# Attention scores made one tile further ahead, normalisations at the head of a step, halves of unit 0 at its end

## The chip, the cores and the metric

One core of one Trainium2 chip runs the whole program; inputs and outputs lie in device memory. The metric is the device time of one execution in microseconds (us), the median of several runs. Engines, in the names of the profile: PE multiplies matrices, DVE (VectorE) and ACT (ScalarE) work elementwise and can reach PSUM, POOL (GpSimd) works elementwise in SBUF only, SP issues the DMAs. Each takes its instructions in the order in which the program lists them, and semaphores hold an instruction until what it needs is there.

## The reference

```
k_sum = max over 32 keys;  v_sum = mean over 32 values          (24 blocks)
scores_l = q k^T / 8 where |i-j| < 16, else -1e9
scores_s = q k_sum^T / 8 + log 32
a = softmax(concat(scores_l, scores_s));  x = a @ concat(v, v_sum)
x = MoE(x)   8 experts, relu MLP 512-1024-512, gates by 8 Sinkhorn rounds
y = (P(h)/Q(h)) @ w_out,  h = x @ w_in                          1536 tokens
```

Batch 2, 8 heads, 768 positions, head size 64, all float32.

## The kernel before, in words

The first 105 us or so are the attention, run as a software pipeline over 24 tiles of 64 queries (a tile has all 8 heads). The loop at line 866 has steps `s` = 0 to 26. A tile `t` goes through these helpers:

- `scores(t)` (L605): 16 small PE products into the PSUM tile `sc` (one buffer), then four DVE reductions that add the mask and keep each row's minimum (L631). It reads the keys of slot `t` in `kw` and four tiles' queries in `qs`, of which there are two buffers.
- `exps(t)` (L637): four ACT exponentials with row sums.
- `norm(t)` (L645): DVE adds 1e-9 (L651), takes the reciprocal (L652), multiplies (L653). The two small results lie in a spare corner of the newest `xo` PSUM tile up to tile 16, and in the SBUF tile `sm` from tile 17.
- `trans(t)` (L655): four PE transposes, one ACT copy to `aT` (pool `att`, two buffers).
- `av(t)` (L669): 16 PE products into `xo` (one PSUM buffer; tiles 1 and 3 use another pool), then ACT writes `xh` (L687) and DVE `xl` (L688). Then `load_vx` asks SP for the values of tile t+3.

Step `s` of the loop issues scores of tile s, av of tile s-3, trans of tile s-2, norm of tile s-1, exps of tile s. Then follows a list of jobs due at that step (`todo`): transposes and copies of later queries and keys (`prep_q` at steps 6, 10, 14, 18; `prep_k` at 7, 8, 9), keys' block maxima on DVE (`block_keys`, L480, steps 8 to 10), copies of them by POOL into the slots of tiles 12 to 15 (`blocks_to`, step 10), weight splitting on ACT and POOL (`split_w2`, steps 8 and 9), and block means of v. From step 7 on, each step also gets one or two "halves" (`mains`, `share`): six PE products each of the first MoE unit on tokens that are already through; two halves of one step stand apart in steps 7 to 11 (one after `av`, one at the end). The ACT and DVE work of a finished pair waits in `posts` and is issued by `flush` after the next `av`. In steps 3 to 5 `spin(3)` issues three dummy PE products whose result nobody reads.

After the loop come the remaining products of the MoE and the last layer, in an order fixed by the program. The block from L866 to L901 is the one that the change rewrites:

```
if s<NQ: scores(s)          # L869
av(s-AV); load_vx; flush()  # L885
trans(s-AV+1); norm(s-1)    # L891, L895
exps(s); todo; main         # L897
```

Of the kernel before, what the change touches and what calls it, by code (L numbers as in the profile page):

```python
# [22 lines left out]
def kernel(  # L23
# [14 lines left out]
    nc = tc.nc  # L38
    B, H, S, D = q.shape
    NT, DM = out.shape  # L40
    NE, _, FE = w1.shape
# [12 lines left out]
    QT = 64  # L54
    NQ = NT // QT
    QB = S // QT
    BLK, WIN = 32, 16
    NB = S // BLK
    WK = QT + 2 * WIN
    SO = 96  # L60
    CO = SO + NB
    NP = H // 2
    LT = 2 * P
    NL = S // LT
# [301 lines left out]
    with ExitStack() as actx:  # L366
# [4 lines left out]
        NS = 16  # L371
        kw = a1.tile([P, NS, NP, CO], F32, name="kw")
        vx = [a1.tile([CO, DM], F32, name=f"vx{i}") for i in range(3)]
        qs = [a1.tile([P, NP, LT], F32, name=f"qs{i}") for i in range(2)]
        wavg = a1.tile([P, 2 * NB], F32, name="wavg")
# [3 lines left out]
        nat = {}  # L379
        kT = {}  # L380
        ks = {}
        vs = {}
        qT = {}
        st = {}
        vps = {}
# [144 lines left out]
        def prep_q(b, i):  # L530
            new_q(b, i)
            for par in range(2):
                place(qT[b, i], par, transpose8("q", b, i, par), qscale, (b, i) == (0, 2))

        def spin(n):

            ps = psm.tile([P, 512], F32, tag="mm", name=f"spin_{len(spins)}")
            spins.append(n)
            for i in range(n):
                nc.tensor.matmul(ps[:, 0:P], lhsT=ident, rhs=ident, start=True, stop=True)  # L540
# [6 lines left out]
            nc.gpsimd.tensor_add(s, t[:, :, 0, :], t[:, :, 1, :])  # L547
            nat["vsum", b, i] = s

        def prep_v(b, *parts):  # L550
            if parts[0] == 0:
                vps[b] = psm.tile([P, DM], F32, tag="mm", name=f"vps_{b}")
            ps = vps[b]
            nb = LT // BLK
            for i in parts:
                o = (NB - nb) - nb * i
                if i == NL - 1:
                    t = nat.pop(("v", b, i))
                    rs_ = [t[:, :, y, :] for y in range(2)]
                else:  # L560
                    rs_ = [nat.pop(("vsum", b, i))]
                for n, r in enumerate(rs_):
                    nc.tensor.matmul(
                        ps[SO:SO + NB, :].rearrange("p (h d) -> p h d", h=H), lhsT=wavg[:, o:o + NB], rhs=r,
                        start=(i == 0), stop=n == 1, tile_position=(0, SO),
                    )
            if parts[-1] == NL - 1:
                nc.vector.tensor_copy(vx[0][SO:SO + NB, :], ps[SO:SO + NB, :])
                vs[b] = vx[0]

        def means_split(i):
            x = nat.pop(("vsum", 1, i)).rearrange("p h d -> p (h d)")
# [23 lines left out]
        def load_vx(t):  # L596
            b, r = divmod(t, QB)
            lo, hi = r * QT - WIN, r * QT + QT + WIN
            c0, c1 = max(lo, 0), min(hi, S)
            nc.sync.dma_start(  # L600
                vx[t % 3][c0 - lo:c1 - lo, :].rearrange("p (h d) -> p h d", h=H),
                v[b, :, c0:c1, :].rearrange("h p d -> p h d"),
            )

        def scores(t):  # L605
            b, r = divmod(t, QB)
            qt = qT[b, r // TPL]
            if t == 1:
                ps = [psa.tile([P, NP, P], F32, tag="tr", name=f"sc_{t}_{x}", bufs=2) for x in range(2)]
            else:  # L610
                ps = psa.tile([P, 2, NP, P], F32, tag="sc", name=f"sc_{t}")
                ps = [ps[:, x] for x in range(2)]
            w = kw[:, slot(t)]
            i = 0 if r == 0 else (2 if r == QB - 1 else 1)
            m = masks[i]
            o = r % TPL * QT
            for p in range(NP):
                x = p % 2
                p = x * (NP // 2) + p // 2
                for j in range(2):  # L620
                    h = slice(j * D, (j + 1) * D)
                    y = (j ^ x) * D
                    nc.tensor.matmul(
                        ps[x][y:y + D, p % (NP // 2), 0:CO], lhsT=qt[h, p, o:o + QT], rhs=w[h, p, :],
                        start=True, stop=True, tile_position=(j * D, y),
                    )
            a = apool.tile([P, NP, CO], F32, tag="a", name=f"a_{t}", bufs=3)
            sm = apool.tile([P, 4, NP], F32, tag="sm", name=f"sm_{t}", bufs=3)
            for p in range(NP):
                p = p % 2 * (NP // 2) + p // 2  # L630
                nc.vector.tensor_tensor_reduce(  # L631
                    out=a[:, p, :], in0=ps[p // (NP // 2)][:, p % (NP // 2), 0:CO], in1=m[:, 0, :],
                    scale=-1.0, scalar=3.0e38, op0=ALU.add, op1=ALU.min, accum_out=sm[:, 0, p:p + 1],
                )
            st[t] = (a, sm, a)

        def exps(t):  # L637
            a, sm, x = st[t]
            for p in range(NP):
                p = p % 2 * (NP // 2) + p // 2  # L640
                nc.scalar.activation(
                    a[:, p, :], x[:, p, :], AF.Exp, scale=-1.0, bias=sm[:, 0, p:p + 1], accum_out=sm[:, 1, p:p + 1]
                )

        def norm(t):  # L645
            a, sm, _ = st[t]
            e, r = sm[:, 2, :], sm[:, 3, :]
            if t < NS + 1:
                o = st["xo"]
                e, r = o[:, 0, QT:QT + NP], o[:, 1, QT:QT + NP]  # L650
            nc.vector.tensor_scalar_add(e, sm[:, 1, :], 1e-9)  # L651
            nc.vector.reciprocal(r, e)  # L652
            nc.vector.tensor_mul(a, a, r.unsqueeze(2).to_broadcast([P, NP, CO]))  # L653

        def trans(t):  # L655
            a = st.pop(t)[0]
            ps = psa.tile([P, NP * P], F32, tag="tr", name=f"at_{t}", bufs=2)
            for p in range(NP):
                nc.tensor.transpose(ps[0:CO, p * P:(p + 1) * P], a[:, p, :], ident)
            aT = apool.tile([CO, NP * P], F32, tag="aT", name=f"aT_{t}")  # L660
            nc.scalar.copy(aT, ps[0:CO, :])
            st[t, "aT"] = aT
# [6 lines left out]
        def av(t):  # L669
            aT = st.pop((t, "aT"))  # L670
            if t < 4 and t % 2:
                ps = psm.tile([P, NP * P], F32, tag="mm", name=f"xo_{t}").rearrange("p (c n) -> p c n", c=NP)
            else:
                ps = psa.tile([P, NP, P], F32, tag="xo", name=f"xo_{t}")
            for p in range(NP):
                for j in range(2):
                    y = p * P + (j ^ (p >= NP // 2)) * QT
                    nc.tensor.matmul(  # L678
                        ps[j * D:(j + 1) * D, p, 0:QT],
                        lhsT=vx[t % 3][:, (2 * p + j) * D:(2 * p + j + 1) * D],  # L680
                        rhs=aT[:, y:y + QT],
                        start=True, stop=True,
                    )
            st["xo"] = ps
            o = t * QT
            dh, dl = xh[:, :, o:o + QT], xl[:, :, o:o + QT]
            nc.scalar.copy(dh, ps[:, :, 0:QT])  # L687
            nc.vector.tensor_sub(dl, ps[:, :, 0:QT], dh.bitcast(F32))  # L688
# [158 lines left out]
        AV = 3  # L847
        mains = []
# [7 lines left out]
                    mains.append((ready, 0, f, NCH, h))  # L856
        share = dict(zip(range(7, 26), (2, 2, 2, 2, 2, 2, 2, 2, 2, 2, 1, 1, 2, 2, 2, 1, 1, 2, 2)))

        def main(s, end):
            n = share.get(s, 0)  # L860
            apart = n == 2 and s < QB
            for _ in range((1 if apart else n) if end else int(apart)):
                assert mains[0][0] <= s
                mains.pop(0)[2]()

        for s in range(NQ + AV):  # L866
            if s == 2:
                norm(0)
            if s < NQ:  # L869
                scores(s)  # L870
            if s == 2:
                prep_v(0, 0)
                prep_v(0, 1)
                norm(1)
                exps(2)
                trans(0)
                by_token_half(0)
                by_token_half(1)
            if s == AV:
                trans(1)  # L880
                exps(3)
                norm(2)
                prep_v(0, 2)
                prep_q(0, 1)
            if s >= AV:  # L885
                av(s - AV)
                if s - AV + 3 < NQ:
                    load_vx(s - AV + 3)
                flush()
            main(s, False)  # L890
            if AV < s < NQ + AV - 1:  # L891
                trans(s - AV + 1)
            if 2 < s < 6:
                spin(3)
            if AV < s <= NQ:  # L895
                norm(s - 1)
            if s < NQ and s not in (2, AV):  # L897
                exps(s)
            for f in todo.pop(s, []):
                f()  # L900
            main(s, True)  # L901
        assert not todo
        flush()
        assert not mains[0][4]
# [88 lines left out]
    for src, dst in ((w_in, f_in), (w_out, f_out)):  # L993
        rows, cols = dst[0].shape[0] // P, dst[0].shape[1]
        flat, o = rows * cols, 0
        while o < flat:
            e = min(o + CW, flat)
# [461 lines left out]
```

## Time and profile before

| | us |
|---|---|
| median of 3 runs (1351.87 to 1351.96) | 1351.94 |
| the profiled execution | 1352.21 |
| its span, first to last instruction | 1350.5 |

| engine | busy us | share |
|---|---|---|
| PE | 1342.1 | 99% |
| DVE | 1052.9 | 78% |
| POOL | 804.3 | 60% |
| ACT | 510.9 | 38% |

The times of the rows further down are microseconds from the start of the span. In a row of the timeline stand start, busy time, engine, line, operation, output and inputs, and how many instructions were merged; in brackets how long the engine was idle before and what ended that. The end of a PE product is modelled, so neighbouring PE rows overlap: what PE gives to a group is read from one start to the next.

### The profile page before, as it was taken

The numbers are of one execution on the slowest core, as the hardware profiler recorded it, in microseconds if no ns is written. First come the engines' busy times: TensorE is split into PE (matmuls) and PEld (weight loads), VectorE is DVE, ScalarE is ACT, GpSimd is POOL, SyncE is SP. The second block draws the span as 40 slices with busy tenths as digits, with TensorE's granted clock in tenths as the row PEclk, the third lists the DMA queues.
The fourth block names the chain that finished last, engine by engine and source line by source line (L and its number), as shares of the span: only waits on it lengthen the run. The fifth ranks groups of instructions, "written<-read, shape, count | busy, mean of one in ns | idle before, by whom it ended". The sixth has DMA issues, their size and how long they took to land.

```text
span 1350.5 us, 20263 instructions
## 1 busy us (share of the span) xinstructions
PE 1342.1 (99%) x7343; PEld 1186.0 (88%) x7343; DVE 1052.9 (78%) x1956; ACT 510.9 (38%) x1136; POOL 804.3 (60%) x983
## 2 busy tenths in 40 slices
PE   8999999999999999999999999999999999999999
PEld 6888898999999999999999999999999888888887
DVE  7775588777777777777787777777777689988885
ACT  6874313222222222222222222222222379866662
POOL 7625747777776777776777767777777012222221
PEclk9999999999999999999999999999999999999999
DMA  9730112222222222222222222222222411312102
GB/s 262 169 85 1 51 46 63 89 70 79 67 73 68 67 77 67 83 66 87 69 77 72 67 74 68 76 69 77 75 80 62 146 57 47 94 33 94 32 16 78
DMA packets 122004, 102.40 MB, mean 76 GB/s; under 512 B 36272, under 2 KB 102960, under 8 KB 121904
## 3 DMA queue, kind: packets, MB, share of 16 engines
q1 hardware_dynamic: 121904, 101.10, 25.7%
q8 instruction: 58, 0.95, 0.3%
q14 instruction: 42, 0.34, 0.1%
HBM read 81.15 MB, written 19.92 MB: 75 GB/s over the span
## 4 chain that ended last, share of the span: by engine, by line
PE 97%; DVE 1%; DMA 1%; ACT 0%; SPq 0%; issue 0%; POOL 0%; DVEq 0%; ACTq 0%
PE p_v L185 12%; PE p_v L184 12%; PE p_v L186 12%; PE p L184 8%; PE p L186 8%; PE p L185 8%; PE X L1234 6%; PE X L1232 6%; PE X L1233 6%; PE Z L1233 3%; PE Z L1234 3%; PE Z L1232 3%; PE Y L1234 2%; PE Y L1233 2%; PE Y L1232 2%; PE xo L678 1%
## 5 line engine op out<-in xcount | busy, mean ns | idle before, releaser
L1347 DVE SCALAR_TENSOR_TENSOR accs<-p_v,Pt,accs 128x512 f32<-128x512 f32 x336 | 244.4, 746 | 85.9 <-PE p_v L186 85.2
L184 PE MATMUL p_v<-w2h_v,hh_v 128*128 128x512 f32 x720 | 282.2, 392 | 0.1
L186 PE MATMUL p_v<-w2h_v,hl_v 128*128 128x512 f32 x720 | 281.9, 392 | 0.0
L185 PE MATMUL p_v<-w2l_v,hh_v 128*128 128x512 f32 x720 | 281.7, 391 | 0.0
L1241 DVE SCALAR_TENSOR_TENSOR hl_v<-s,hh_v 128x384 fp32r<-128x384 f32 x180 | 137.4, 763 | 76.0 <-ACT hh_v L1240 74.6
L234 POOL TENSOR_TENSOR hl<-ta,hh 128x512 fp32r<-128x512 f32 x48 | 62.5, 1302 | 204.4 <-ACT hh L233 150.0
L1252 ACT COPY s<-X 128x384 f32<-128x384 f32 x56 | 27.0, 482 | 406.6 <-PE X L1234 406.6
L1041 POOL TENSOR_SCALAR ce<-ce 128x296 uint32<-128x296 uint32 (+1 forms) x56 | 67.1, 1199 | 176.7 <-DVE ce L1032 176.7
L186 PEld LDWEIGHTS p_v<-w2h_v,hl_v 128*128 128x128 f32 x720 | 135.2, 188 | 28.3
L184 PEld LDWEIGHTS p_v<-w2h_v,hh_v 128*128 128x128 f32 x720 | 135.4, 188 | 26.3 <-DVE accs L1342 0.5
L185 PEld LDWEIGHTS p_v<-w2l_v,hh_v 128*128 128x128 f32 x720 | 135.3, 188 | 25.9
L1240 ACT ACTIVATE hh_v<-s 128x384 fp32r<-128x384 f32 x180 | 94.9, 527 | 126.8 <-DVE s L1275 68.6
L110 POOL TENSOR_TENSOR wS<-S,wS 128x256 fp32r<-128x256 f32 x120 | 100.2, 835 | 14.4 <-ACT wS L107 4.7
L184 PE MATMUL p<-xh,w1h 128*128 128x512 f32 (+2 forms) x272 | 100.8, 371 | 0.0
L186 PE MATMUL p<-xh,w1l 128*128 128x512 f32 (+2 forms) x272 | 99.1, 364 | 0.0
L185 PE MATMUL p<-xl,w1h 128*128 128x512 f32 (+2 forms) x272 | 99.1, 364 | 0.0
L184 PE MATMUL p<-w2h,hh 128*128 128x512 f32 (+1 forms) x240 | 94.0, 392 | 0.0
L186 PE MATMUL p<-w2h,hl 128*128 128x512 f32 (+1 forms) x240 | 93.3, 389 | 0.0
L185 PE MATMUL p<-w2l,hh 128*128 128x512 f32 (+1 forms) x240 | 93.2, 388 | 0.0
L110 POOL TENSOR_TENSOR w2l_v<-sb,w2h_v 128x512 fp32r<-128x512 f32 x60 | 82.9, 1382 | 5.0
L1234 PE MATMUL X<-th,wS 128*128 128x384 f32 x240 | 80.3, 335 | 0.0
L1232 PE MATMUL X<-th,wS 128*128 128x384 f32 x240 | 80.3, 335 | 0.0
(249 smaller groups left out, 3309.1 us busy)
## 6 DMA issues: line engine op xcount, KB each, us to landing
sa<-in_moe_w_dram SPq DMA_DIRECT2D x30, 512.0 KB, 3.4
sb<-in_moe_w_dram SPq DMA_DIRECT2D x30, 512.0 KB, 4.3
cv<-in_moe_w_in_dram SPq DMA_DIRECT2D x24, 296.0 KB, 2.9
w1h<-f_in SPq DMA_DIRECT2D x16, 256.0 KB, 2.8
w1l<-f_in SPq DMA_DIRECT2D x16, 256.0 KB, 3.2
w2h<-f_out SPq DMA_DIRECT2D x16, 256.0 KB, 4.9
w2l<-f_out SPq DMA_DIRECT2D x16, 256.0 KB, 5.1
vx<-in_v_dram SPq DMA_DIRECT2D x20, 192.0 KB, 4.2
```

Of the source, the lines that this page charges most:

```text
L110: nc.gpsimd.tensor_sub(lo, src, hi.bitcast(F32))
L184: nc.tensor.matmul(ps, lhsT=sh, rhs=mh, start=(i == 0), stop=False)
L185: nc.tensor.matmul(ps, lhsT=sh, rhs=ml, start=False, stop=False)
L186: nc.tensor.matmul(ps, lhsT=sl, rhs=mh, start=False, stop=(i == n_k - 1))
L234: nc.gpsimd.tensor_sub(hl[:, :n], ta, hh[:, :n].bitcast(F32))
L1041: nc.gpsimd.tensor_scalar(out=e, in0=e, scalar1=896, scalar2=0, op0=ALU.subtract, op1=ALU.max)
L1232: nc.tensor.matmul(ps, lhsT=w[:, 0, t], rhs=mh, start=start and t == 0, stop=False, **go)
L1233: nc.tensor.matmul(ps, lhsT=w[:, 0, t], rhs=ml, start=False, stop=False, **go)
L1234: nc.tensor.matmul(ps, lhsT=w[:, 1, t], rhs=mh, start=False, stop=t == 1, **go)
L1240: nc.scalar.activation(hh, src, AF.Relu)
L1241: nc.vector.scalar_tensor_tensor(out=hl, in0=src, scalar=0.0, in1=hh.bitcast(F32), op0=ALU.max, op1=ALU.subtract)
L1347: nc.vector.scalar_tensor_tensor(out=a, in0=ps, scalar=Pt[:, g, e:e + 1], in1=a, op0=ALU.mult, op1=ALU.add)
```

## The change

Tile t = s+1 (from step 4 on; tile 4 joins tile 3 in step 3) gets its scores and exponentials in step s. `norm(s-1)` and `trans(s-2)` move to the head of the step, ahead of scores and av. Both halves of a step stand at its end. Two tiles of av are done in step 4 and none in step 3; the last block-mean product of batch 0 is issued in two parts around `scores(4)`; the queries of tiles 4 to 7 are prepared ahead of the exponentials of tile 3; `spin` runs in steps 4 and 5 alone. `norm` uses the corner of `xo` for every tile.

```diff
+        def mean_rows(ps, i, r, **flags): ...   # one block-mean product, as before
+        def prep_v_end(y):
+            ps = vps[0]
+            mean_rows(ps, NL - 1, nat["v", 0, NL - 1][:, :, y, :], start=False, stop=y == 1)
+            if y:
                 nc.vector.tensor_copy(vx[0][SO:SO + NB, :], ps[SO:SO + NB, :])
...
         def norm(t):
-            e, r = sm[:, 2, :], sm[:, 3, :]
-            if t < NS + 1:
-                o = st["xo"]
-                e, r = o[:, 0, QT:QT + NP], o[:, 1, QT:QT + NP]
+            o = st["xo"]
+            e, r = o[:, 0, QT:QT + NP], o[:, 1, QT:QT + NP]
...
-        def main(s, end): ...
         for s in range(NQ + AV):
             if s == 2:
                 norm(0)
-            if s < NQ:
-                scores(s)
-            if s == 2:
+            if AV < s <= NQ:
+                norm(s - 1)
+            if AV + 1 < s < NQ + AV - 1:
+                trans(s - AV + 1)
+            t = s if s <= AV else s + 1
+            if t < NQ:
+                scores(t)
+            if s < 2:
+                exps(s)
+            elif s == 2:
                 prep_v(0, 0)
...
-            if s == AV:
+            elif s == AV:
                 trans(1)
+                prep_q(0, 1)
                 exps(3)
+                prep_v_end(0)
                 norm(2)
-                prep_v(0, 2)
-                prep_q(0, 1)
-            if s >= AV:
-                av(s - AV)
-                if s - AV + 3 < NQ:
-                    load_vx(s - AV + 3)
+                scores(4)
+                prep_v_end(1)
+                exps(4)
+                trans(2)
+            else:
+                for i in range(s - AV if s > AV + 1 else 0, s - AV + 1):
+                    av(i)
+                    if i + 3 < NQ:
+                        load_vx(i + 3)
                 flush()
-            main(s, False)
-            if AV < s < NQ + AV - 1:
-                trans(s - AV + 1)
-            if 2 < s < 6:
-                spin(3)
-            if AV < s <= NQ:
-                norm(s - 1)
-            if s < NQ and s not in (2, AV):
-                exps(s)
+                if s < 6:
+                    spin(3)
+                if t < NQ:
+                    exps(t)
             for f in todo.pop(s, []):
                 f()
-            main(s, True)
+            for _ in range(share.get(s, 0)):
+                assert mains[0][0] <= s
+                mains.pop(0)[2]()
```

## Rows read from the trace of the kernel before

**Rows 1.** The page: engines; TensorE's granted clock in 40 slices; the chain that ended last.

```profile
PE 1342.1 (99%) x7343; PEld 1186.0 (88%) x7343; DVE 1052.9 (78%) x1956; ACT 510.9 (38%) x1136; POOL 804.3 (60%) x983
...
PEclk9999999999999999999999999999999999999999
...
PE 97%; DVE 1%; DMA 1%; ACT 0%; SPq 0%; issue 0%; POOL 0%; DVEq 0%; ACTq 0%
```

**Rows 2.** Waits of PE over the whole span: total us, times, longest us.

```profile
PE at L659 <- ACT a L641: 0.3, 1, 0.3
```

**Rows 3.** Timeline of PE, first steps of the loop.

```profile
1.42 4.64 PE L540 MATMUL spin<-ident 128*128 128x128 f32 x20 [1.42 <-POOL ident masks.py:199]
...
22.25 0.69 PE L678 MATMUL xo<-aT,vx 120*64 120x64 f32 x16
22.86 0.94 PE L540 MATMUL spin<-ident 128*128 128x128 f32 x6
23.73 0.64 PE L623 MATMUL sc<-kw,qs 64*64 64x120 f32 x16
24.30 0.69 PE L678 MATMUL xo<-aT,vx 120*64 120x64 f32 x16
24.91 0.65 PE L659 MATMUL at<-ident,a 128*120 128x128 f32 x4
25.40 0.83 PE L540 MATMUL spin<-ident 128*128 128x128 f32 x6
...
35.56 0.64 PE L623 MATMUL sc<-kw,qs 64*64 64x120 f32 x16
...
39.68 0.64 PE L623 MATMUL sc<-kw,qs 64*64 64x120 f32 x16
```

**Rows 4.** Timeline of ACT, step 6 and the head of step 7.

```profile
30.54 0.59 ACT L661 COPY aT<-at 120x512 f32<-120x512 f32 x1
31.02 0.40 ACT L641 ACTIVATE a<-a,sm 128x120 f32<-128x120 f32 x1
...
32.55 1.13 ACT L440 ACTIVATE qs<-qps 128x512 f32<-128x512 f32 x2
33.56 0.36 ACT L687 CAST xh<-xo 128x256 fp32r<-128x256 f32 x1
```

**Rows 5.** Timeline of DVE, step 10.

```profile
46.42 0.42 DVE L688 TENSOR_TENSOR xl<-xo,xh 128x256 fp32r<-128x256 f32 x1
...
47.09 0.15 DVE L651 TENSOR_SCALAR xo<-sm 128x4 f32<-128x4 f32 x1
...
48.07 1.21 DVE L480 TENSOR_REDUCE ks<-kw 128x32 f32<-128x1024 f32 x1
49.20 0.68 DVE L438 TENSOR_SCALAR qs<-qps 128x512 f32<-128x512 f32 x1
49.80 0.27 DVE L631 CUSTOM_DVE_ANT_0 a<-sc,mask 128x120 f32<-128x120 f32 x1
```

**Rows 6.** Timelines of ACT, POOL and PE, from step 9 to step 12.

```profile
44.91 1.12 ACT L107 CAST w2h<-s 128x512 fp32r<-128x512 f32 x2
...
45.59 2.54 POOL L110 TENSOR_TENSOR w2l<-s,w2h 128x512 fp32r<-128x512 f32 x2 [0.53 <-ACT w2h L107]
...
50.37 0.53 POOL L388 TENSOR_SCALAR kw<-ks 128x384 f32<-128x384 f32 x1
...
52.53 0.64 PE L623 MATMUL sc<-kw,qs 64*64 64x120 f32 x16
```

**Rows 7.** Timelines of PE and DVE, steps 22 and 23.

```profile
90.81 0.69 PE L678 MATMUL xo<-aT,vx 120*64 120x64 f32 x16
...
93.29 0.69 PE L678 MATMUL xo<-aT,vx 120*64 120x64 f32 x16
...
91.94 0.42 DVE L688 TENSOR_TENSOR xl<-xo,xh 128x256 fp32r<-128x256 f32 x1
...
93.02 0.66 DVE L653 TENSOR_TENSOR a<-a,sm 128x480 f32<-128x480 f32 x1
```

More of the change, by code (lines that the diff above doesn't have):

```diff
@@ L548, in sum_v, with mean_rows, prep_v @@
             nat["vsum", b, i] = s
-        def prep_v(b, *parts):
-            if parts[0] == 0:
-                vps[b] = psm.tile([P, DM], F32, tag="mm", name=f"vps_{b}")
[L553 to L567, printed above, removed]
+        def mean_rows(ps, i, r, **flags):
+            nb = LT // BLK
+            o = (NB - nb) - nb * i
+            nc.tensor.matmul(
+                ps[SO:SO + NB, :].rearrange("p (h d) -> p h d", h=H), lhsT=wavg[:, o:o + NB], rhs=r,
+                tile_position=(0, SO), **flags,
+            )
+        def prep_v(b, i):
+            if i == 0:
+                vps[b] = psm.tile([P, DM], F32, tag="mm", name=f"vps_{b}")
+            mean_rows(vps[b], i, nat.pop(("vsum", b, i)), start=i == 0, stop=False)
+        def prep_v_end(y):
+            ps = vps[0]
+            mean_rows(ps, NL - 1, nat["v", 0, NL - 1][:, :, y, :], start=False, stop=y == 1)
+            if y:
                 nc.vector.tensor_copy(vx[0][SO:SO + NB, :], ps[SO:SO + NB, :])
-                vs[b] = vx[0]
+                vs[0] = vx[0]
         def means_split(i):
@@ L857 @@
         share = dict(zip(range(7, 26), (2, 2, 2, 2, 2, 2, 2, 2, 2, 2, 1, 1, 2, 2, 2, 1, 1, 2, 2)))
[L859 to L864, printed above, removed]
         for s in range(NQ + AV):
```

## The prediction, made before the change was built

> **What bounds the kernel now.** I read the page first, then the waits of PE, then the timelines of PE, DVE, ACT and POOL through the attention. The page shows PE busy 99% of the span, the chain that ended last lying 97% on PE, and the granted clock at its full level in every slice [rows 1]. The waits of PE name 0.3 at the end of the loop [rows 2]. The timeline shows why: from step 3 on each group of PE products starts where the one before lets go [rows 3]. PE's list is as long before as after, so the change gains only what PE now spends on waiting and dummies, and loses whatever hole the new order tears. A hole in the attention isn't made up later, because PE has no slack after it. The sum is therefore one of holes, made against the profiled 1352.21 (span 1350.5); that execution lies 0.27 above the median.
>
> **What can be gained.** One of three dummy groups goes: 23.73 - 22.86 = 0.87 [rows 3]. The hole ahead of the first av (22.25 less 0.25) and the waits of PE at the end of the loop (0.3, [rows 2]) may go: 0.55. So about 1.4. Merging the halves saves one change of shape in steps 7 to 11, a twentieth of a microsecond each, but puts scores behind transposes in all later steps; I take 0 for both, with bounds of -0.2 and +0.6.
>
> **What the new order asks of the other engines.** Scores one tile earlier need their inputs one step earlier, and three of those inputs are made by jobs that stay in their old step. So I laid the new lists of each engine side by side and followed the wait that ends last in each step.
>
> *Start, up to scores(8).* Scores(8) moves from step 8 to step 7. Its queries are transposed at the end of step 6 and copied by ACT, both halves, behind exps: before, behind exps(6); now behind exps(7). ACT's list can be counted from av(0). Before, av(0) starts at 22.25. Now scores(4), trans(2) and scores(5) come ahead of it, 0.57 + 0.49 + 0.57 [rows 3] and 0.1 lead-in each, and the transposes of the queries wait for their copy by 0.5; the hole of 0.25 is filled: 24.35. The third `aT` has no buffer until av(0) has read the first, so ACT goes on at 24.35 + 0.61 + 0.15 = 25.1. Then up to the end of the query copies: three `aT` copies of 0.48, the exponentials of tiles 5 to 7, 3 x 1.53, four `xh` of about 0.3, and the two query copies, 1.01 by the starts 30.54, 31.02, 32.55 and 33.56 [rows 4]: 1.44 + 4.59 + 1.2 + 1.0 = 8.2, so 33.3 without a wait. I add 1.0 for waits on av(2), av(3) and on the reductions of tile 7, which now stand behind norm(5) on DVE; bounds 0 and 1.6. Scores(8) can start at about 34.4. PE is ready sooner: from 24.35 it has av(0) to av(3), 4 x 0.61, two dummy groups of 0.77, trans(3) to trans(5), 3 x 0.5, scores(6) and (7), 2 x 0.66, eight transposes, 0.9: 7.7, so 32.1. The hole is 2.3 (1.2 to 2.9). When scores(8) has ended, at 35.0, PE still owes what it had done before scores(8) in the kernel before: av(4), the transposes of the keys and two halves, 0.61 + 0.9 + 1.5 = 3.0, so 38.0 against 35.56 + 0.57 = 36.13 [rows 3]. The start loses **1.8**, bounds 0.7 and 2.5: the dummy and the old holes are already in it.
>
> *Steps 9 to 11.* The single `xo` buffer makes av wait until the last norm that used its corner is done. That norm was issued ahead of the step's jobs; now it comes after them, at the head of the next step. DVE's list between two av's is then the `xl`, the `hl` of the posts, block_keys, the copy of keys or queries and the norm, in whatever order 49.80 - 46.42 = 3.38 [rows 5], and it starts 1.13 after the av (90.81 to 91.94 in [rows 7]): 4.5, with hand-overs 4.6 to 4.7. PE needs 39.68 - 35.56 = 4.12 for such a step [rows 3], a little less in the new order (4.0). Hole: 0.7 in step 9 (0.4 to 0.8).
>
> The next holes, av(7) in step 10 and scores(12) in step 11, share one end. Scores(12) needs the block maxima in its slot, which POOL copies last in a list that starts from ACT's second `w2h` pair: from 45.59 to 50.37 + 0.53, 5.31 [rows 6]. Before, scores(12) came at 52.53, 1.6 after that. Now it comes about a step sooner. From av(6) in step 9: ACT waits for it (0.76), then `xh` and `hh`, some 0.3 each, exponentials 1.53, key copy 0.53, first cast 0.65: 4.1; POOL 5.3; hand-overs 0.1: 9.5. PE has from av(6) to scores(12) two steps of 4.0 less the av to scores part, 7.4. Together **2.1**, however it splits, and with step 9 **2.8**. Bounds: ACT ran later than this in the kernel before (w2h 4.66 after that av, not 3.45), which adds up to 1.2; if POOL's sum of values finds a place earlier it is 1.3 less.
>
> *Later query copies* (scores 16 and 20, steps 15 and 19): after the transposes PE has two halves and a trans, 2.0 or more, ACT and DVE by then no backlog. 0, at most 0.3.
>
> *Steps 23 and 24.* These have one half each and no scores any more. From av to the end of the next norm DVE and ACT need 93.02 + 0.66 - 90.81 = 2.87 [rows 7], with `hl`; 2.6 without. Before, norms used `sm` from tile 17 on, and av came 93.29 - 90.81 = 2.48 after the last one. Now the norm holds the `xo` buffer, and without scores PE asks after 1.9. Holes 1.0 and 0.8, **1.8**; the waits that rows 2 show, **-0.3**, go with the norm at the head.
>
> Moved DMAs: SP now issues the load of the first keys of batch 1 ahead of two value loads, not between them, so it goes out sooner, the value loads 2 later and three steps ahead of their use. I take 0.
>
> **Sum.** 1.8 + 2.8 + 1.8 - 0.3 = 6.1; 1352.21 + 6.1 - 0.27 = 1358.0.
>
> **Clock.** The granted clock shows the full level (2.4 GHz) throughout [rows 1], though the first twenty dummies took 4.64 where six took 0.83 later [rows 3]. The Trainium skill, TensorE: Matmul & The Clock Gate, section "HAM oscillation — how this bites in real kernels", says that idle gaps of PE can put the clock back to its lower level. The hole ahead of scores(8) would be the longest of the loop. The rule would make it a rival of its own, the third below.
>
> **Rivals.**
> 1. *The look-ahead hides what it should (not slower).* If ACT's backlog isn't there, exps(7) and the query copies done before PE has finished trans(5), at 32.1, and the block copy is done before step 11, then no hole opens and the gain above stands: 1352.21 - 1.4 - 0.27 = 1350.5. It decides at scores(8). For it: every producer is one step ahead, and ACT idles in steps 3 and 4 before. Against it: 8.2 of ACT work between av(0) and scores(8) where PE has 7.7, and POOL's list ending 1.6 before the old place of scores(12). Chance 0.14.
> 2. *Norm does not hold av up.* If the corner of `xo` is released sooner than I think, the 0.7 and 1.8 go, while the common end of scores(12) stays: 1358.0 - 2.5 = 1355.5. For it: no row before shows such a wait; against it: one buffer. Chance 0.15.
> 3. *The hole costs clock too.* If the level falls to 1.2 GHz after the hole and comes back as at the start, where twenty dummies lost 4.64 - 20 x 0.83/6 = 1.9: 1359.9. Against it: the hole is half as long as that stretch of dummies, and no slice of the trace shows a granted clock below the full level. Chance 0.07.
>
> **How the numbers follow.** The forecast has 0.58; its own range is 1355.5 to 1360.5, from the bounds above. Something that I don't see, of either sign, has 0.06. A change of 0.2% is 2.7 us, about what a measurement tells here; slower begins at 1354.6, faster at 1349.2. Slower: 0.55 of the forecast, 0.12 of rival 2, 0.07 of rival 3, 0.01 of the rest: 0.75. Rival 1 is mostly no change: 0.09, with 0.10 from the others' edges: 0.19. Faster: 0.06. The range leaves out rival 1 and a little above: 1353.5 to 1361.0.
>
> **What would show it.** In the changed kernel's timeline PE should stand idle before scores(8) at about 32 to 34.4, with ACT's query copies ending just then; before av(6), with the multiply of a norm ending just then; before scores(12), with POOL's copy of `ks` ending just then; and before the last av's but two, behind L653. The slot of 30 to 35 us should show PE busy less than it is now. If PE has no idle row there and the scores of tile 8 start before 33, the step on ACT's backlog is wrong, and with it the sign.

## The result, and the profile after

The changed kernel takes 1362.13 us (median of 5 runs, 1359.67 to 1362.40) where the kernel before takes 1351.96: 1.0071 times as long by the means of the runs, 95% interval 1.0057 to 1.0085. It is slower, as predicted, but by 10.2 (medians) and not by 6. Its runs differ with the mean granted clock that they show: 1359.67 at 1.000, 1361.14 at 0.999, 1362.13, 1362.21 and 1362.40 at 0.997. The profiled execution is the 1362.40 one, span 1360.7. The clock goes with the time: the run at 1.000 is 2.73 shorter than the profiled one.

The page of the changed kernel, the same three parts as [rows 1]:

```profile
PE 1345.4 (99%) x7337; PEld 1187.8 (87%) x7337; DVE 1050.4 (77%) x1956; ACT 511.9 (38%) x1136; POOL 804.3 (59%) x983
...
PEclk9899999999999999999999999999999999999999
...
PE 95%; DVE 2%; DMA 1%; ACT 1%; issue 0%; SPq 0%; POOL 0%; ACTq 0%; DVEq 0%
```

Two things are new: PE's share of the chain falls from 97% to 95%, so other engines now end waits that matter, and the second slice of the granted clock is an 8. PE's busy time is 3.3 longer although one group of three dummies (six instructions) is gone.

Waits of PE in the loop of the changed kernel, which the kernel before doesn't have (engine, line, waited for: total us, times, longest); two shorter ones, of 0.63 and 0.44, stand in the timeline below:

```profile
PE sc L622 <- ACT qs L440: 2.2, 1, 2.2
...
PE xo L675 <- PE sc L622: 1.1, 2, 0.6
PE xo L675 <- ACT a L640: 1.1, 1, 1.1
PE sc L622 <- DVE a L650: 1.1, 1, 1.1
...
PE xo L675 <- ACT aT L658: 0.9, 1, 0.9
```

**The start.** Timelines of PE, ACT, DVE and POOL of the changed kernel, up to trans(6); answers to [rows 3] and [rows 4]:

```profile
24.71 1.15 PE L675 MATMUL xo<-aT,vx 120*64 120x64 f32 x32 [0.63 <-DVE a L650]
...
32.55 0.62 PE L656 MATMUL at<-ident,a 128*120 128x128 f32 x4 [0.44 <-DVE a L650]
35.34 1.08 PE L622 MATMUL sc<-kw,qs 64*64 64x120 f32 x16 [2.17 <-ACT qs L440]
...
40.45 0.41 PE L184 MATMUL p<-xh,w1h 128*128 128x256 f32 x1
40.66 0.41 PE L185 MATMUL p<-xl,w1h 128*128 128x256 f32 x1
...
41.63 0.60 PE L656 MATMUL at<-ident,a 128*120 128x128 f32 x4
...
25.79 0.59 ACT L658 COPY aT<-at 120x512 f32<-120x512 f32 x1 [1.74 <-PE xo L675]
...
32.64 0.40 ACT L640 ACTIVATE a<-a,sm 128x120 f32<-128x120 f32 x1 [1.14 <-DVE sm L630]
...
34.17 1.12 ACT L440 ACTIVATE qs<-qps 128x512 f32<-128x512 f32 x2
...
24.00 0.65 DVE L650 TENSOR_TENSOR a<-a,xo_r 128x480 f32<-128x480 f32 x1
...
29.62 1.80 DVE L145 TENSOR_TENSOR w1l<-s,w1h 128x512 fp32r<-128x512 f32 x1
...
29.59 1.28 POOL L145 TENSOR_TENSOR w1l<-s,w1h 128x512 fp32r<-128x512 f32 x1
```

Scores(8) starts at 35.34 after 2.17 of idling, and the query copies end at 34.17 + 1.12 = 35.29: the predicted hole, with the predicted releaser. What then follows is not on time. Products that the kernel before starts every 0.12 start every 0.21 here (40.45 to 40.66). The windows of the changed kernel say why (start and end; length; busy time of PE, PEld, DVE, ACT and POOL; granted clock; DMA share; GB/s):

```profile
32.00:34.00 2.00, 0.73 (x5) 0.41 (x4) 1.91 (x12) 1.36 (x7) 2.00 (x3) 1.00 1.05 313
34.00:35.00 1.00, 0.00 (x0) 0.00 (x0) 0.65 (x1) 1.00 (x4) 1.00 (x3) 0.84 1.24 226
35.00:36.00 1.00, 0.66 (x14) 0.66 (x16) 0.00 (x0) 0.74 (x2) 1.00 (x2) 0.50 1.18 276
...
41.00:42.00 1.00, 1.00 (x9) 0.99 (x7) 0.00 (x0) 0.00 (x0) 1.00 (x3) 0.75 0.91 276
42.00:43.00 1.00, 1.00 (x27) 0.68 (x26) 0.13 (x1) 0.59 (x1) 0.35 (x1) 1.00 1.08 390
```

While PE idles ahead of scores(8) the granted clock goes from 1.00 to 0.50 (1.2 GHz instead of 2.4), stays there through the six microseconds of work after the hole (0.50 in every microsecond from 35 to 41), and is back before 42. The work from scores(8) to trans(6), 35.34 to 41.63, takes 6.29.

**The rest of the loop.** PE, DVE and POOL of the changed kernel, later; answers to [rows 5 to 7]:

```profile
47.44 0.69 PE L675 MATMUL xo<-aT,vx 120*64 120x64 f32 x16 [0.56 <-PE sc L622]
...
52.13 0.69 PE L675 MATMUL xo<-aT,vx 120*64 120x64 f32 x16 [0.54 <-PE sc L622]
...
56.76 0.64 PE L622 MATMUL sc<-kw,qs 64*64 64x120 f32 x16 [1.06 <-DVE a L650]
...
103.16 0.69 PE L675 MATMUL xo<-aT,vx 120*64 120x64 f32 x16 [1.10 <-ACT a L640]
...
106.08 0.69 PE L675 MATMUL xo<-aT,vx 120*64 120x64 f32 x16 [0.89 <-ACT aT L658]
...
112.33 0.69 PE L675 MATMUL xo<-aT,vx 120*64 120x64 f32 x16
...
46.68 0.65 DVE L650 TENSOR_TENSOR a<-a,xo 128x480 f32<-128x480 f32 x1
...
102.25 0.65 DVE L650 TENSOR_TENSOR a<-a,xo 128x480 f32<-128x480 f32 x1
...
46.73 2.52 POOL L110 TENSOR_TENSOR w2l<-accs,w2h 128x512 fp32r<-128x512 f32 x2 [4.37 <-ACT w2h L107]
...
56.21 0.50 POOL L388 TENSOR_SCALAR kw<-ks 128x384 f32<-128x384 f32 x1
```

Av(6), av(7), scores(12), av(20) and av(21) wait where they were expected to. The releaser in the brackets is inferred, and for the av's it misses: av(6) at 47.44 starts when the multiply of a norm ends, 46.68 + 0.65 = 47.33, and av(20) at 103.16 when the one at 102.25 has ended. Both read the corner of the `xo` buffer into which av writes. Scores(12) at 56.76 follows POOL's copy, 56.21 + 0.50. The multiply of a norm on DVE ends at the same moment (56.07 + 0.65), so this trace alone doesn't tell which it waits for. In y1_sm8 below it starts at 52.01, when POOL's copy has ended (51.45 + 0.51) and the multiply still runs (51.56 + 0.90): it is POOL's copy.

**Where the 10.2 lies.** All of it is in the loop. The last av of the kernel before:

```profile
102.17 0.69 PE L678 MATMUL xo<-aT,vx 120*64 120x64 f32 x16
```

From the last av (112.33) to the end of the span there are 1248.4, in the kernel before 1248.3. At the start of trans(6) PE has done what it had done at 36.13 in the kernel before (when av(5) started), but for one dummy group; it is 5.50 later. The same work from scores(8) to trans(6) takes 3.54 at full clock in a run shown below, so 6.29 - 3.54 = 2.75 of that is clock, which fits the 2.73 between the runs, and 2.75 is the start itself. From there to the last av the changed kernel needs 70.70, the kernel before 66.04: 4.66. Sum 2.75 + 2.75 + 4.66 = 10.16.

### The profile page after: what moved, and what is told of

The parts are those of the page before. It is cut to its first block, busy times and chain, and to the rows that moved or that the text cites. A ratio compares the mean times of both kernels' runs of the same rounds, so it can differ in the third digit from the quotient of the medians.

```text
span 1360.7 us, 20254 instructions
## 1 busy us (share of the span) xinstructions
PE 1345.4 (99%) x7337; PEld 1187.8 (87%) x7337; DVE 1050.4 (77%) x1956; ACT 511.9 (38%) x1136; POOL 804.3 (59%) x983
## 4 chain that ended last, share of the span: by engine, by line
PE 95%; DVE 2%; DMA 1%; ACT 1%; issue 0%; SPq 0%; POOL 0%; ACTq 0%; DVEq 0%
PE p_v L185 12%; PE p_v L186 12%; PE p_v L184 12%; PE p L184 8%; PE p L186 8%; PE p L185 8%; PE X L1233 6%; PE X L1231 6%; PE X L1232 6%; PE Z L1233 3%; PE Z L1232 3%; PE Z L1231 3%; PE Y L1233 2%; PE Y L1232 2%; PE Y L1231 2%; PE xo L675 1%
## 5 line engine op out<-in xcount | busy, mean ns | idle before, releaser
L1240 DVE SCALAR_TENSOR_TENSOR hl_v<-s,hh_v 128x384 fp32r<-128x384 f32 x180 | 134.6, 748 | 75.8 <-ACT hh_v L1239 74.6
L1233 PE MATMUL X<-th,wS 128*128 128x384 f32 x240 | 80.2, 334 | 0.0
L1232 PE MATMUL X<-tl,wS 128*128 128x384 f32 x240 | 80.2, 334 | 0.0
```

The costliest lines, as they stand in the source:

```text
L1232: nc.tensor.matmul(ps, lhsT=w[:, 0, t], rhs=ml, start=False, stop=False, **go)
L1233: nc.tensor.matmul(ps, lhsT=w[:, 1, t], rhs=mh, start=False, stop=t == 1, **go)
L1240: nc.vector.scalar_tensor_tensor(out=hl, in0=src, scalar=0.0, in1=hh.bitcast(F32), op0=ALU.max, op1=ALU.subtract)
```

## The experiments

Those named x, and y1, y2, z1, z2 and z5, are edits of the changed kernel; y3, y4 and z4 are edits of the kernel before. The kernel before took 1351.85 to 1351.91 (medians) beside them.

**x1_fill: dummies in the hole**, ten products that nobody reads (20 instructions in the rows), ahead of scores(8).

```diff
+            if s == 7:
+                spin(10)
             if t < NQ:
```

> Ten dummy products (20 rows, about 2.2 us) stand ahead of the scores of tile 8, in the hole in which PE waits for ACT's query copies. Nothing else changes. Theory A (the idle hole lets TensorE's clock fall, and that costs 2.8 on top of the holes): scores(8) still starts at about 35.3, no slice shows a granted clock below the full level, all runs lie close together at 1362.1 - 2.8 = 1359.3 (1358.9 to 1359.9). Rival B (the clock falls because steps 3 to 6 have fewer dummies and more pauses, or for a reason outside this stretch): 36 to 41 us is still at half the clock, 1362 as before.

Measured: 1359.80 (1359.55 to 1360.01), clock 1.000 in all five runs; ratio 1.0059 (1.0046 to 1.0071). PE in x1_fill:

```profile
33.36 2.40 PE L540 MATMUL spin<-ident 128*128 128x128 f32 x20
35.70 0.64 PE L622 MATMUL sc<-kw,qs 64*64 64x120 f32 x16
...
39.25 0.60 PE L656 MATMUL at<-ident,a 128*120 128x128 f32 x4
```

Scores(8) comes 0.36 later than in the changed kernel, and trans(6) 2.38 earlier: 3.55 for the same work. Work without a use, put into an idle stretch, gains 2.3, so the clock loss is real and the idle stretch causes it. The time is that of the changed kernel's run at 1.000, 1359.67.

**x2_spin3: more work ten microseconds ahead of the hole.** Three dummies after trans(2) in step 3, the hole untouched.

```diff
                 exps(4)
                 trans(2)
+                spin(3)
```

> One group of three dummy products (0.8 us) goes back into step 3, behind trans(2), where the kernel before has a group; scores(8) still waits for its queries. Theory A: the group fills part of a pause at 24 us, the hole at 33 us stays, the clock falls in it as in the changed kernel in most runs: 1361 to 1363. Rival B (the missing group is why the clock falls): granted clock full throughout, 1359.3.

Measured: 1359.82 and 1359.87 at clock 1.000, 1361.02 and 1361.38 at 0.999; ratio 1.0066 (1.0050 to 1.0081). The hole is still 2.16. Neither expectation fits whole: with the same hole the clock fell in two of four runs and, by their mean clock, for a shorter time. The changed kernel too held 1.000 in one of its five runs and had one at 0.999, so two falls of four against four of five don't show that the dummies helped. The same program with the same hole falls in some runs and not in others; what else decides stays open.

**x3_queries: the query copies ahead of exps(7).**

```diff
+                if s == 6:
+                    prep_q(0, 2)
                 if t < NQ:
                     exps(t)
...
-        ... for j in range(2, NQ // TPL)]
+        ... for j in range(3, NQ // TPL)]
```

> In step 6 the transposes and copies of the queries of tiles 8 to 11 are issued ahead of the exponentials of tile 7 instead of behind them. Theory A with the forecast's step on ACT's backlog: ACT is idle for 1.1 before those exponentials anyway, so the copies end at about 32.8, the hole of 2.2 ahead of scores(8) closes to under 0.3, the clock stays at its full level: 1362.1 - 2.1 - 2.8 = 1357.2 (1356.5 to 1358). Rival C (ACT and DVE are the bound of steps 4 to 8 and a wait only changes its place): the exponentials of tile 7 come later, trans or norm waits for them, 1359 or more.

Measured: 1357.69 (1357.54 to 1357.96), clock 1.000 in all five; ratio 1.0043 (1.0031 to 1.0056). PE in x3_queries:

```profile
33.56 0.64 PE L622 MATMUL sc<-kw,qs 64*64 64x120 f32 x16 [0.18 <-ACT a L640]
```

The hole is 0.18. Taking its cause away gives 4.4: 2.1 more than filling it. That shows the ACT order (exps(7) ahead of the copies) as the cause of hole and clock loss both.

**x4_sm17: norm results in `sm` from tile 17 on**, as before the change.

```diff
-            o = st["xo"]
-            e, r = o[:, 0, QT:QT + NP], o[:, 1, QT:QT + NP]
+            e, r = sm[:, 2, :], sm[:, 3, :]
+            if t < 17:
+                o = st["xo"]
+                e, r = o[:, 0, QT:QT + NP], o[:, 1, QT:QT + NP]
```

> From tile 17 on the two small results of a normalisation go to the SBUF tile sm again, as in the kernel before; tiles up to 16 keep the corner of xo. Theory A (the single xo buffer holds av until the norm that used its corner is done): the holes ahead of av(20) and av(21), 1.10 and 0.89, shrink to 0.3 together: 1.7 less, 1360.4 where the clock falls at 34 us as in the changed kernel, 1357.9 where it doesn't. Rival D (these two av wait for ACT's copies, as the wait rows of the changed kernel name ACT): the holes stay, same time as the changed kernel.

Measured: 1357.73 in the one run at clock 1.000 (the profiled one), 1359.21 to 1360.77 in the four at 0.997 to 0.999. Against the changed kernel's run at 1.000 that is 1.9 less (one run each), at 0.997 it is some 1.5 less (1360.71 and 1360.77 against 1362.13 to 1362.40), and the waits of av(20) and av(21), 1.99 together, are gone but for 0.16. PE in x4_sm17, and then its windows:

```profile
35.22 0.64 PE L622 MATMUL sc<-kw,qs 64*64 64x120 f32 x16 [2.16 <-ACT qs L440]
...
38.76 0.60 PE L658 MATMUL at<-ident,a 128*120 128x128 f32 x4
```

```profile
33.00:35.00 2.00, 0.06 (x1) 0.00 (x0) 1.45 (x6) 2.00 (x9) 2.00 (x3) 1.00 1.13 300
35.00:37.00 2.00, 1.78 (x37) 1.56 (x38) 0.97 (x9) 1.10 (x4) 2.00 (x3) 1.00 0.81 195
```

The same hole, and in this execution the clock held: this gives the 3.54 used above.

**y1_sm8: x3_queries with `sm` from tile 8 on** (`t < 8` in the lines above).

> On top of the queries ahead (1357.7): from tile 8 on the two small results of a normalisation go to the SBUF tile sm, so that no av from av(5) on waits for a norm through the xo buffer. Theory A (that buffer is the wait): no hole ahead of av(6) and av(7), 0.55 each now, nor 1.1 and 0.9 at the end; scores(12) still waits for POOL's block copy, whose list starts from av(6), so of the first two only about 0.6 comes off: 1357.7 - 0.6 - 1.8 = 1355.3 (1354.8 to 1356). Rival D: the waits come back at the same places through ACT or DVE, or the norms beside POOL's work become so much slower with sm (1.34 instead of 0.65 for the multiply in the kernel before) that trans waits for them: 1357 or more.

Measured: 1355.59 to 1355.87 in three runs at clock 1.000, 1357.20 to 1357.87 in three at 0.999; ratio 1.0033 (1.0021 to 1.0045). The waits of av(6), av(7), av(20) and av(21), 3.1 together, are gone but for 0.15: it was the corner of `xo` that held them. But scores(12) now waits 2.10 instead of 1.06, so at full clock only 2.1 is left, and in half of the runs the clock falls behind that hole. PE, DVE and POOL in y1_sm8:

```profile
52.01 0.86 PE L622 MATMUL sc<-kw,qs 64*64 64x120 f32 x16 [2.10 <-POOL kw L388]
...
46.28 1.76 DVE L652 TENSOR_TENSOR a<-a,sm 128x480 f32<-128x480 f32 x1
...
46.24 2.95 POOL L110 TENSOR_TENSOR w2l<-s,w2h 128x512 fp32r<-128x512 f32 x2
```

The multiply that takes 0.65 from `xo` (46.68 in the changed kernel, beside POOL's pair at 46.73) takes 1.76 from `sm` beside POOL's tensor_tensor, and POOL's pair 2.95 instead of 2.52 (2.54 in [rows 6]). This is the cost that the corner of `xo` avoids in the first 17 tiles.

**y2_order: y1_sm8, with one weight split on DVE later and a sum of values on POOL one step later.**

```diff
-        W1 = [(4, 5), (4, 5),
+        W1 = [(4, 6), (4, 5),
...
-            at(9 + i, sum_v, 1, i)
+            at(10 + i, sum_v, 1, i)
```

> The kernel with queries ahead and sm from tile 8, and two jobs a step later: DVE's low part of the first w1 chunk in step 6 (it took 1.80 beside POOL's like work, ahead of norm(5) and the reductions of tile 7), POOL's sums of v of batch 1 from step 10 on, behind the block copy that scores(12) wait for. Theory A: the 0.4 ahead of trans(5) goes, and the hole ahead of scores(12), 1.1 to 1.6, shrinks to 0.3: 1355.3 - 0.4 - 1.1 = 1353.8 (1353 to 1354.5). Rival E (POOL's late sums delay the block means of step 13 and scores or the means product wait there instead): 1355.

Measured: 1354.55 (1354.31 to 1354.86, 11 runs, clock 1.000 in all); ratio 1.0020 (1.0011 to 1.0028). PE and POOL in y2_order:

```profile
50.91 0.64 PE L622 MATMUL sc<-kw,qs 64*64 64x120 f32 x16 [1.48 <-DVE sm L650]
...
50.25 0.51 POOL L388 TENSOR_SCALAR kw<-ks 128x384 f32<-128x384 f32 x1 [0.48 <-DVE ks L480]
```

This is just above the first expectation, because the hole ahead of scores(12) shrank only from 2.10 to 1.48. POOL's copy now waits for the block maxima on DVE: with POOL's list shortened, DVE is next, and its list carries another multiply of 1.75. DVE's copy of the queries of the same tile ends together with POOL's copy (50.09 + 0.68 and 50.25 + 0.51). By its median this is the best version that keeps the look-ahead, 2.6 over the kernel before.

**z1_allq: y2_order with every later query preparation ahead of the exponentials.**

```diff
+                if s in (6, 10, 14, 18):
+                    prep_q(*divmod((s + 2) // TPL, NL))
                 if t < NQ:
                     exps(t)
```

> On top of the kernel with two jobs a step later (1354.55): the transposes and copies of all later queries (steps 6, 10, 14, 18) go ahead of the exponentials of their step, and so, on DVE, ahead of block_keys in step 10. Theory A (each early set of scores waits for whichever input was made last): the hole ahead of scores(12), 1.48, shrinks to what POOL's block copy still needs, 0.3 to 0.6: 1353.5 (1353.2 to 1354). Rival E (block_keys, now behind the query copy, delays POOL's block copy by as much): 1354.3 or more.

Measured: 1355.08 and 1355.69 at clock 1.000, 1356.48 to 1356.85 in three at 0.999; ratio 1.0032 (1.0019 to 1.0045). A miss for the first expectation; the rival E came true. Both runs at 1.000 are dearer than all eleven of y2_order. DVE and POOL in z1_allq:

```profile
49.29 0.68 DVE L438 TENSOR_SCALAR qs<-qps 128x512 f32<-128x512 f32 x1
49.89 1.20 DVE L480 TENSOR_REDUCE ks<-kw 128x32 f32<-128x1024 f32 x1
...
51.17 0.51 POOL L388 TENSOR_SCALAR kw<-ks 128x384 f32<-128x384 f32 x1 [1.06 <-DVE sm L650]
```

The query copy of step 10 moved ahead of the block maxima on DVE as well, so POOL's copy for scores(12) starts 0.92 later than in y2_order (0.33 of it z1_allq lags already at scores(11)), and the hole grows from 1.48 to 1.98. The copies for scores(16) and (20) had nothing to gain, as predicted.

**z2_nodummy: z1_allq without the dummies in steps 4 and 5.**

```diff
-                if s < 6:
-                    spin(3)
```

> The kernel with all queries ahead, without its two groups of dummy products (they compute nothing). Theory A (ACT sets the pace of steps 4 and 5; dummies delay scores there a little, as in the kernel before, where leaving them out gave 0.45): 0.2 to 0.6 less than with them, about 1353.1, clock full. Rival B: the pauses of 0.7 let the clock fall, 1355 in some runs.

Measured: 1354.60 to 1354.77 in three runs at clock 1.000, 1356.06 to 1356.88 in four at 0.999; ratio 1.0028 (1.0017 to 1.0039). Some 0.3 to 0.7 less than z1_allq at the same clock, with few runs; the hole ahead of scores(12) is again 1.98.

**z4_normhead: the kernel before, with norm and trans at the head of a step and no look-ahead.**

```diff
+            if AV < s <= NQ:
+                norm(s - 1)
+            if AV < s < NQ + AV - 1:
+                trans(s - AV + 1)
             if s < NQ:
                 scores(s)
```

(and the same four lines taken away behind av).

> The kernel before with one part of the change alone: norm(s-1) and trans(s-2) at the head of the step from step 4 on, no look-ahead of the scores. Theory A: av waits for norm through xo, and norm at the head waits for exps of the step before, so a step can't be shorter than av, xh, hh, exps, norm in a row, 0.76 + 0.3 + 0.3 + 1.53 + 1.05 and hand-overs, about 4.1. Steps of 4.1 and more lose little, those of 2.5 to 3.2 (4 to 6, 15 to 18, 20 to 23) lose 0.9 to 1.6 each: 1360 to 1366. Rival G (the place of norm is harmless, the look-ahead alone makes the holes): 1352 to 1353.

Measured: 1357.99 (1357.89 to 1358.08), clock 1.000 in all four; ratio 1.0045 (1.0030 to 1.0061). Waits of PE in z4_normhead:

```profile
PE xo L678 <- PE sc L623: 2.1, 4, 0.6
PE xo L678 <- DVE sm L631: 1.9, 2, 0.9
```

Between the two expectations: +6.1. Four av's in steps 8 to 11 wait 0.5 to 0.6 and two later ones 0.93 and 0.94, 4.0 in all. Without the look-ahead the `xo` buffer is held just the same, so this part of the loss needs only the norm at the head. No hole stands ahead of scores(8), and the clock holds.

**z5_normback: x3_queries with the norm behind av and flush.**

```diff
-            if AV < s <= NQ:
-                norm(s - 1)
...
                 flush()
+                if s <= NQ:
+                    norm(s - 1)
```

> The kernel with the queries of tiles 8 to 11 ahead (1357.7), and norm(s-1) put back behind av and its posts, as in the kernel before; small results in xo for every tile. Theory A (the holes ahead of av come from norm standing behind the step's jobs on DVE, at the head of the next step): no holes ahead of av(6) and av(7), those at the end 0.5 or less, while scores(12) waits up to 2.1 for POOL's block copy, with a fall of the clock in some runs: 1355.0 to 1357.5, 1355.5 where the clock stays. Rival D: av waits there as before, 1357.7.

Measured: 1365.72 (1365.63 to 1365.96), clock 1.000 in all four; ratio 1.0103 (1.0089 to 1.0117). A plain miss, 8.0 over x3_queries. Waits of PE in z5_normback:

```profile
PE at L656 <- DVE a L650: 8.9, 10, 1.6
PE sc L622 <- POOL kw L388: 1.5, 1, 1.5
```

No av waits for a norm any more; the transposes do, ten times by this row: at the start of the loop, where a step has no halves yet (1.60 and 1.18), and from 76 us on. With trans at the head of the next step, the norm behind av must be done within the rest of the step, and there PE has too little to do meanwhile. Norm at the head is thus the cheaper place once trans stands at the head.

**y3_halves: the kernel before with both halves at the end of a step.**

```diff
-    apart = n == 2 and s < QB
+    apart = False
```

> The kernel before with one part of the change alone: both halves of a step at its end in steps 7 to 11. Theory A (order of PE's groups is worth a twentieth of a microsecond a step, nothing waits for it): 1351.95 - 0.25 = 1351.7 (1351.4 to 1352.1). Rival F (the half between av and trans covers a wait for norm or for the copy of aT, and without it PE waits): 1352.5 or more.

Measured: 1351.97 (1351.81 to 1352.18, 11 runs); ratio 1.0001 (0.9992 to 1.0009): nothing, as the prediction had it.

**y4_nodummy: the kernel before without `spin(3)` in steps 3 to 5.**

```diff
-            if 2 < s < 6:
-                spin(3)
```

> The kernel before without its three groups of dummy products in steps 3 to 5 (they compute nothing). Theory A (the clock falls only in an idle stretch as long as the one ahead of scores(8) in the changed kernel, over 2 us): pauses of 0.8 three times, clock full, ACT sets the pace there: 1351.3 to 1352.0. Rival B (these pauses, closer together, are enough for the clock to fall): a slice below the full level around 25 to 35 us, 1353 or more in some runs.

Measured: 1351.46 (1351.17 to 1351.71, 11 runs, clock 1.000 in all); ratio 0.9996 (0.9987 to 1.0005). Waits of PE in y4_nodummy:

```profile
PE sc L623 <- DVE sm L631: 0.6, 2, 0.3
...
PE at L659 <- DVE a L653: 0.4, 1, 0.4
```

Of three groups of 0.87 only some 0.45 comes back, because PE then waits 0.2 to 0.4 at a time, mostly for DVE. It is the lowest time of all versions, though by the interval it can't be told from the kernel before.

## Why the prediction was right in its sign and wrong in its size

- **PE bound, holes not made up: right.** What follows the loop takes 1248.3 in both kernels.
- **Start up to scores(8): right in place and releaser, sized 1.8, measured 2.75.** The hole is 2.17 (2.3 predicted), scores(8) starts at 35.34 (34.4 predicted), exps(7) waits 1.14 (1.0 predicted for such waits). What was missed comes earlier. Av(0) starts at 24.71, not 24.35 (the terms given for it add up to 24.43), behind a hole of 0.63 that was to be filled: the multiply of norm(2) ends at 24.00 + 0.65, and its corner `xo_r` lies in the same single `xo` buffer, so the wait that was foreseen for step 9 comes in step 4 already. ACT's `aT` copy starts at 25.79, when av(1) has ended too and the next PE row starts, 0.32 later after av(0) than counted; why it waits for both isn't shown. These two make some 0.7 of the 0.9 by which scores(8) is late. The wait of 1.14 fits the allowance of 1.0, but mostly by a cause that the prediction doesn't have, so that is in part luck. DVE's weight split at 29.62 takes 1.80, in the kernel before 0.99, since it now meets POOL's tensor_tensor at 29.59; that delays norm(5), so trans(5) waits 0.44, and the reductions of tile 7, for which exps(7) waits (1.14 less 0.81 would be 0.33, an estimate). In y2_order the same split, moved to 32.0, takes 0.69, and the scores of tile 8 come 0.47 earlier than in y1_sm8; it was not moved alone. The Trainium skill, SBUF — State Buffer, section "Who interferes with whom", says that a DVE instruction with two SBUF inputs contends with a GpSimd instruction that reads SBUF, while one with at most one SBUF input, outside DVE's two-port modes, does not. These rows and the multiply of y1_sm8 (1.76 from `sm`, 0.65 from `xo`) agree.
- **Clock: the step that failed.** The sum was made with the full level throughout; the fall was a rival with a chance of 0.07 and a price of 1.9. It happened in four of five runs and cost 2.75 in the profiled one; the one run that kept 1.000, 1359.67, lies inside the stated range. The price was taken from the twenty dummies of [rows 3], 4.64 long; the stretch at half level after the hole is about 6.3 long. (Over those dummies the windows of the trace show a granted clock of 1.00, so that the clock made them slow isn't shown.) The argument against it (a hole half as long as that stretch, and no slice below full level) compared with a trace that has no such hole in it. x1_fill, where the hole is filled, and x3_queries, where it is taken away, both keep 1.000 in every run. The Trainium skill, TensorE: Matmul & The Clock Gate, section "HAM oscillation — how this bites in real kernels", the source of that rival, says that an idle gap of PE can put its clock back to the lower level. These runs agree in kind, but the gap that it warns of is longer than the 2.17 that was enough here, and x4_sm17 shows an execution with the same hole and no fall.
- **Steps 9 to 11: right in mechanism, 2.8 predicted, 0.56 + 0.54 + 1.06 = 2.16 measured.** The norm holds av through `xo` (y1_sm8 and z4_normhead show it from both sides), which rules out rival 2, and scores(12) starts at the end of POOL's copy. Rival 1, no hole at all, is out by the first row of the waits.
- **Steps 23 and 24: 1.8 predicted, 1.10 + 0.89 = 1.99 measured**, and x4_sm17 gives back 1.5 to 1.9.
- **The -0.3: misread.** The wait of [rows 2] isn't at the end of the loop. It stands at 18.64, in step 2 of the kernel before, and PE's timeline has no idle row from there to the last av:

```profile
18.64 0.62 PE L659 MATMUL at<-ident,a 128*120 128x128 f32 x4 [0.25 <-ACT a L641]
```

- **Small terms.** The 4.66 from trans(6) to the last av is 2.16 + 1.99 = 4.15 of waits and 0.51 more. The 0.51 is the new order of PE's groups, read from start to start over this stretch in both timelines, waits left out: the 18 groups of trans, now right ahead of scores or av, take 9.78 where they took 7.55, the halves 31.35 where they took 33.12, and the other groups together 0.05 more. The prediction took 0 for it, with bounds of -0.2 and +0.6. z4_normhead, with the same trans ahead of scores, loses more than its waits tell too; the place of trans was not tried alone. The order of the halves is worth 0 (y3_halves). A dummy group, counted as a gain of 0.87 where it goes, is worth about 0.15 (y4_nodummy): the pauses that it covered come up in its place.
- **Range.** Its upper end, 1361.0, priced the terms but not the clock on top of an undersized start: with 1.8 and 0 for 2.75 and 2.75, 3.7 of the 4.1 between the prediction and the median are accounted for.

## What to carry to other kernels

Where PE bounds a stage, price an idle stretch of some 2 us twice: once as waiting, and once as the work behind it at half clock, from rows at both levels. Making one product of a software pipeline earlier gained nothing here, in no version (1354.55 at best against 1351.91): PE had little to gain, and whenever one input came sooner, another copy or a shared buffer became the last to be ready. Follow each moved job to the next reader of its buffer. Before moving an elementwise job in time, look at what runs beside it on the engine next to it.

## What was not expected of the hardware

- The granted clock fell at a hole of 2.17 in most runs of the changed kernel, in the profiled one while PE still idled (0.84 in 34 to 35 us), and stayed low for about 6.3 of work. In y1_sm8 it still read 1.00 in 51 to 52 us and fell in 52 to 53 (0.65), when the scores behind the hole of 2.10 had begun at 52.01. It doesn't fall in all runs: with holes of 1.98 to 2.17 runs at 1.000 and at 0.997 to 0.999 stand side by side (x2_spin3, x4_sm17, y1_sm8, z1_allq, z2_nodummy), and with holes of 1.48 and 1.60 at most all eleven runs of y2_order and all four of z5_normback held 1.000.
- A DVE tensor_tensor with two SBUF inputs took 1.76 to 1.80 beside a tensor_tensor of POOL, where its likes take 0.65 to 0.99; with one input in PSUM it kept its 0.65 beside the same POOL work.
